# Two transformer layers on one core: aligned activation parts, a three-tile rotation for the last score pairs, and an output projection cut in two

## The chip, the cores and the metric

The kernel runs on one core of a Trainium2 chip. The metric is the device time of one execution in microseconds (us). Three runs of the kernel before gave 3531.59, 3531.69 and 3532.29 us; the median, 3531.69, stands for it below.

## The reference

Two identical layers work on a sequence of 2048 tokens with 512 features. Both layers use the same weights.

```python
# attention: 32 heads of 16 features
qkv = layernorm(x) @ wqkv                       # 512 x 1536
p = softmax(q @ k.T / sqrt(16)); o = p @ v
x = x + o.reshape(B, S, D) @ wo                 # 512 x 512
# MLP with Mish, hidden size 1792
h = layernorm(x) @ w1 + b1
x = x + (h * tanh(softplus(h))) @ w2
```

All of it is float32, and the softmax is a true one, with the maximum of each row taken off.

## The kernel before

**Precision.** The kernel gets float32 accuracy from a faster matmul form by splitting operands: each is a high part (rounded by a copy to the type `F32R`) and a low part (the rest). A product is three matmuls: high by high, high by low, low by high. `mm3` (L176 to L181) issues these three; so lines 179, 180 and 181 of the profile stand for the projections `qk`, `va`, `vp`, `wo` and `h`. The second MLP product `mo` issues its three at L724.

**Tiling.** The 2048 tokens are four chunks of 512 (index `c`). A layer runs through these stages:

1. `qkv`: query and key projections (`order` lists which feature block of which chunk comes when), then the value projection of chunks 0 to 2 (`v_parts`, 48 parts of three matmuls).
2. Attention: eight groups of four heads, four query chunks, 16 key tiles make 512 steps (`STEPS`) of four heads each.
3. Output projection `project(c)` of each chunk: 16 parts of three matmuls (`wo_parts`), added to the residual `x2s[c]` on VectorE (DVE) at L685, two row tiles at a time.
4. MLP: for each chunk and each of 14 hidden tiles, `hid(c, f)` computes a 128 x 512 tile of hidden values in 12 matmuls and sends it through ten operations that alternate between ScalarE (ACT) and DVE (L701 to L712); they end in the high part `ah` and the low part `al`. `outp(c, f)` multiplies these by `w2` in 12 matmuls (L724), with slices of `ah` and `al` as the stationary operand and `w2` as the moving one. `outp` trails `hid` by two groups (`LAG = 2`).

**The attention loop.** Per three steps, `CYCLE` holds four `P` (a pair of heads: two score matmuls into a PSUM tile of tag `s2`, one exponential of 128 x 1024 on ACT), four `S` (a single head: one score matmul into the PSUM tile `s1`, one exponential of 128 x 512), four `v` (probabilities by values: a run of narrow `pv` matmuls) and six `M` (the row maxima: two `pm` matmuls into one of two PSUM tiles of tag `mx`, one reduction on DVE at L387). `s2` and `s1` have one buffer each, so a pair's matmuls wait until the exponential of the pair before it has read `s2`. The maxima of a query chunk must be complete before its scores, so `M` runs ahead of `P`: `AHEAD + PRE` = 28 steps of maxima are issued inside stage 1 (`some_max`, after some projections and after every third value part); the first four steps of the loop have value projections of chunk 3 in place of `M`; and `M` is used up 24 steps before the end of the loop. From step 500 on (`FILL = 12`) each step also issues one part of `project(0)`; 16 steps hold all of it.

**What sets the order.** On TensorE the order is that of the code, written out by an explicit chain (`att.pe`). On the other engines a planner places an instruction where it believes its inputs to be ready, also ahead of others that stand before it in the code; `behind(...)` pins an instruction behind everything that its engine has been given so far. DMAs of the SP and POOL queues are issued in the order in which they are placed there, and one that waits holds up those behind it.

**Memory.** `blk` is a pool of 22 buffers of 8 KB per partition; weights, probabilities, residuals and normalised activations rotate through it. `tmp` is a pool of smaller tiles with a fixed place for each tag, in the order of first use. Adding up the sizes of the tiles that come ahead of them: every `blk` buffer starts at a multiple of 512 bytes; the tags `f` and `ah` of `tmp` start 384 bytes past a multiple of 512; `hr`, `he` and `al` start 128 bytes past one.

**The seam between attention and MLP.** After the loop come the loads of the last chunk's heads (`outs[3].load`), of residuals and weights; then `project(1)` with the first normalisation of chunk 0 between its parts, then `project(2)`, then the MLP. The last chunk's heads are divided by their softmax sums and split into parts at the hook of hidden tile 2 (`outs[3].parts(False)`: a multiplication of 128 x 2048 on DVE at L655, a copy on ACT, a subtraction on DVE at L662), and projected at tiles 6 to 9. The normalisations of the later chunks (`spread`, `norm_blocks`, `statistics`: L189, L278, L283 and two DMAs) are spread over hooks from tile 7 of chunk 0 and tile 5 of chunks 1 and 2. Their statistics are not pinned.

Of the kernel before, what the change touches and what calls it, by code (L numbers as in the profile page):

```python
# [18 lines left out]
P = 128  # L19
# [21 lines left out]
AHEAD = 24  # L41
PRE = 4
FILL = 12
# [6 lines left out]
LAG = 2  # L50
MAX_M = (6, 3, 7)
# [17 lines left out]
def kernel(ctx: ExitStack, tc: tile.TileContext, x, wqkv, wo, w1, b1, w2, out):  # L69
# [8 lines left out]
    dram = ctx.enter_context(tc.tile_pool(name="dram", bufs=1, space=DRAM))  # L78

# [103 lines left out]
    def statistics(src, nm):  # L183
        st = tmp.tile([P, NCH, 6], F32, tag="st", name=f"st{nm}")
        mv = tmp.tile([P, NCH, 2], F32, tag="mv", name=f"mv{nm}")
        ve = tmp.tile([P, NCH], F32, tag="ve", name=f"ve{nm}")
        rs = tmp.tile([P, NCH], F32, tag="rs", name=f"rs{nm}")
        for t in range(NCH):
            nc.vector.bn_stats(st[:, t], src[:, t])  # L189
# [114 lines left out]
    class Attention:  # L304
        def __init__(self, l, scr):
# [5 lines left out]
            self.singles, self.full, self.unit = 0, None, 0  # L311
            self.chained, self.last = False, None
# [50 lines left out]
        def max_mm(self, s, half):  # L363
            if s >= STEPS:
                return
# [56 lines left out]
        def pair(self):  # L422
# [4 lines left out]
            sp = self.pool.tile([P, 2, CW], F32, tag="s2", name=f"sp{self.l}{i}")  # L427
# [55 lines left out]
        def run(self, hooks, pre, fill):  # L483
# [3 lines left out]
            with tc.tile_pool(name="sa", bufs=1, space=PSUM, reuse_waits="tile") as self.pool:  # L487
                half, done = 2 * (AHEAD + PRE), -4
                for s in range(STEPS + 4):
# [21 lines left out]
                    if s + FILL >= STEPS:  # L511
                        next(fill, None)
# [21 lines left out]
    def qkv(l, att, wts, tt, order, within, due):  # L534
# [91 lines left out]
    class HeadsOut:  # L626
# [26 lines left out]
        def parts(self, aside):  # L653
# [4 lines left out]
            if aside:  # L658
                nc.gpsimd.tensor_copy(oh, self.num)
            else:  # L660
                nc.scalar.activation(oh, self.num, AF.Copy)
            behind(nc.vector.tensor_tensor(ol, self.num, oh.bitcast(F32), op=ALU.subtract))  # L662
            self.out = oh, ol

    def wo_parts(l, c, outs, wot, x2, pe, paired=True):
        oh, ol = outs[c].out
        for t in range(NCH):
# [15 lines left out]
            if paired and t % 2:  # L683
                x2v = x2[:, t - 1 : t + 1]
                behind(nc.vector.tensor_tensor(x2v, acc, x2v, op=ALU.add))  # L685

    def mlp(l, x2s, w1t, w2t, tts, dst, hooks, pe):
# [27 lines left out]
        def outp(c, f):  # L715
# [5 lines left out]
            turns = zip(*terms) if f == FT - 1 else [terms[0] + terms[1], terms[2]]  # L721
# [75 lines left out]
    for l in range(2):  # L797
# [18 lines left out]
        qkv(l, att, wts, tt, order, within, due)  # L816
        wot, w1t, w2t, x2s, tts = [], [], [], [], {}
# [24 lines left out]
        for i in range(2):  # L842
            at(STEPS - GSTEPS + 2 * i, lambda i=i: wot.append(ready(f"wo{i}", l)))
            at(STEPS - 50 + 2 * i, lambda i=i: load_res(i))
        at(STEPS - GSTEPS + 8, lambda: load_w1(0))
        outs = [HeadsOut(l, c, att.oscr) for c in range(NCH)]
        for c, (t0, t1, t2, t3) in enumerate(((-42, -20, -19, -13), (-26, -19, -18, -11), (-10, -6, -4, 0))):
# [4 lines left out]
            at(STEPS + t3, lambda o=o: o.parts(True))  # L852
# [4 lines left out]
        fill = project(0)  # L857
        att.run(hooks, v_parts(l, NCH - 1, wts, tt, att, True), fill)
# [5 lines left out]
        for _ in fill:  # L864
# [5 lines left out]
        for i, _ in enumerate(project(2)):  # L870
# [12 lines left out]
        on(2, lambda: outs[3].parts(False))  # L883
# [15 lines left out]
        if l == 0:  # L899
            last = NCH - 1  # L900
            for f, js in ((2, (0,)), (4, (2,)), (9, (1,)), (11, (3,)), (12, (4,)), (13, (5,))):
                hooks.setdefault((last, f), []).append(lambda js=js: load_qkv(1, wts, js, splits))
            for c in range(last):
                spread(hooks, last, (1, 5, 8)[c], x2s[c], f"q1{c}", tt, c)
        mlp(l, x2s, w1t, w2t, tts, xs if l == 0 else out, hooks, att.pe)
# [29 lines left out]
```

## Time and profile before

| what | value |
|---|---|
| median of three runs | 3531.69 us |
| profiled execution, its own time | 3532.86 us |
| its span, first to last instruction | 3531.1 us |
| TensorE busy (PE) | 3512.9 us, 28572 matmuls |
| VectorE busy (DVE) | 3002.7 us |
| ScalarE busy (ACT) | 2582.8 us |
| TensorE clock granted, mean | 0.999 |

Times within the profile are microseconds from the start of the span. Layer 0 has its attention loop from 164 to 1419 and its MLP from 1444 to 1777; layer 1 has them from 1920 to 3176 and from 3203 to the end. PE is the matmul stream, PEld the loading of the stationary operand, which runs beside the matmuls. Matmuls overlap in the pipeline: one of 512 columns lasts 389 ns in the profile, but the next one starts about 227 ns after it. So the cost of a matmul is read from one start to the next, not from its duration.

### The profile page before, as it was taken

The numbers are of one execution on the slowest core, as the hardware profiler recorded it, in microseconds if no ns is written. First come the engines' busy times: TensorE is split into PE (matmuls) and PEld (weight loads), VectorE is DVE, ScalarE is ACT, GpSimd is POOL, SyncE is SP. The second block draws the span as 40 slices with busy tenths as digits, with TensorE's granted clock in tenths as the row PEclk, the third lists the DMA queues.
The fourth block names the chain that finished last, engine by engine and source line by source line (L and its number), as shares of the span: only waits on it lengthen the run. The fifth ranks groups of instructions, "written<-read, shape, count | busy, mean of one in ns | idle before, by whom it ended". The sixth has DMA issues, their size and how long they took to land.

```text
span 3531.1 us, 68820 instructions
## 1 busy us (share of the span) xinstructions
PE 3512.9 (99%) x28572; PEld 1922.5 (54%) x28572; DVE 3002.7 (85%) x3160; ACT 2582.8 (73%) x3513; POOL 239.2 (7%) x392
## 2 busy tenths in 40 slices
PE   9999999999999999999999999999999999999999
PEld 7644444444444444788876444444444444447887
DVE  6789999999999994776756999999999999947665
ACT  3288888888888888356622888888888888874665
POOL 3100001010000002100010000000000000021000
PEclk9999999999999999999999999999999999999999
DMA  7641312213131124630364211112121111247100
GB/s 250 228 92 47 83 47 74 61 51 71 43 81 42 49 81 71 207 96 25 111 217 147 48 39 38 38 29 44 31 36 39 41 36 31 79 74 222 66 13 24
DMA packets 182196, 273.97 MB, mean 78 GB/s; under 512 B 67508, under 2 KB 111476, under 8 KB 168060
## 3 DMA queue, kind: packets, MB, share of 16 engines
q1 hardware_dynamic: 154964, 192.91, 21.4%
q10 hardware_dynamic: 19176, 43.06, 3.5%
q0 software_dynamic: 7744, 33.60, 3.4%
q8 instruction: 224, 3.67, 0.4%
q14 instruction: 88, 0.72, 0.1%
HBM read 158.87 MB, written 109.58 MB: 76 GB/s over the span
## 4 chain that ended last, share of the span: by engine, by line
PE 96%; DVE 2%; DMA 1%; issue 1%; ACT 0%; POOL 0%; SPq 0%; DVEq 0%; ACTq 0%; POOLq 0%
PE pv L457 30%; PE pm L383 18%; PE ss L441 13%; PE sp L431 10%; PE mo L724 8%; PE h L179 3%; PE h L181 3%; PE h L180 3%; PE qk L179 2%; PE qk L180 1%; PE qk L181 1%; PE wo L179 1%; PE va L179 1%; PE wo L181 1%; PE wo L180 1%
## 5 line engine op out<-in xcount | busy, mean ns | idle before, releaser
L387 DVE TENSOR_REDUCE mxv<-pm 128x2 f32<-128x1024 f32 x2048 | 2385.2, 1219 | 138.6 <-PE pm L383 88.5
L432 ACT ACTIVATE p<-sp 128x1024 f32<-128x1024 f32 x1366 | 1395.9, 1022 | 19.7 <-PE sp L431 15.3
L457 PE MATMUL pv<-p,va 128*32 128x256 f32 (+2 forms) x16032 | 1166.9, 392 | 0.1
L383 PE MATMUL pm<-ks,qs 48*128 48x512 f32 x4096 | 1096.0, 446 | 0.3
L442 ACT ACTIVATE p<-ss 128x512 f32<-128x512 f32 x1364 | 814.6, 597 | 349.1 <-PE ss L441 263.5
L431 PE MATMUL sp<-qs,ks 50*128 50x512 f32 x2732 | 725.6, 447 | 0.5 <-ACT p L432 0.2
L457 PEld LDWEIGHTS pv<-p,va 128*32 128x32 f32 x16032 | 367.7, 108 | 498.4 <-issue 420.6
L383 PEld LDWEIGHTS pm<-ks,qs 48*128 48x128 f32 x4096 | 449.9, 184 | 345.6 <-issue 216.6
L441 PE MATMUL ss<-qs,ks 50*128 50x512 f32 x1364 | 611.0, 448 | 0.0
L441 PEld LDWEIGHTS ss<-qs,ks 50*128 50x128 f32 x1364 | 252.0, 185 | 329.5 <-ACT p L442 225.5
L431 PEld LDWEIGHTS sp<-qs,ks 50*128 50x128 f32 x2732 | 261.1, 183 | 200.5 <-ACT p L432 119.1
L402 POOL CAST np<-nt 128x32 fp32r<-128x32 f32 x64 | 13.3, 208 | 2213.4 <-DVE nt L400 2213.4
L701 ACT ACTIVATE hb<-h,b1t 128x512 f32<-128x512 f32 x112 | 76.7, 685 | 96.6 <-PE h L181 90.6
L173 ACT ACTIVATE pt<-qk 128x512 fp32r<-128x512 f32 x64 | 38.2, 597 | 143.5 <-PE qk L181 102.9
L705 ACT ACTIVATE hr<-he 128x512 f32<-128x512 f32 x112 | 70.9, 633 | 82.3 <-DVE he L704 82.3
L708 DVE TENSOR_TENSOR hb<-hb,hr 128x512 f32<-128x512 f32 x112 | 77.2, 689 | 51.0 <-ACT hr L706 49.3
L712 DVE TENSOR_TENSOR al<-hb,ah 128x512 fp32r<-128x512 f32 x112 | 77.2, 690 | 36.8 <-ACT ah L711 33.8
L711 ACT ACTIVATE ah<-hb 128x512 fp32r<-128x512 f32 x112 | 70.5, 629 | 50.7 <-DVE hb L708 40.1
L702 DVE TENSOR_SCALAR he<-hb 128x512 f32<-128x512 f32 x112 | 47.5, 424 | 67.0 <-ACT hb L701 61.6
L704 DVE SCALAR_TENSOR_TENSOR he<-he 128x512 f32<-128x512 f32 x112 | 77.0, 687 | 25.4 <-ACT he L703 24.8
L703 ACT ACTIVATE he<-he 128x512 f32<-128x512 f32 x112 | 70.3, 628 | 32.2 <-DVE he L702 32.2
L174 DVE TENSOR_TENSOR pt<-qk,pt 128x512 fp32r<-128x512 f32 x64 | 43.9, 686 | 52.8 <-ACT pt L173 50.7
(235 smaller groups left out, 3081.8 us busy)
## 6 DMA issues: line engine op xcount, KB each, us to landing
scr<-pt ACTq DMA_DIRECT2D x64, 512.0 KB
qs<-scr SPq DMA_DIRECT2D x174, 128.0 KB
ks<-scr SPq DMA_DIRECT2D x174, 128.0 KB
vscr<-v SPq DMA_DIRECT2D x32, 512.0 KB
va<-vscr SPq DMA_DIRECT2D x64, 256.0 KB
oscr<-ot SPq DMA_DIRECT2D x64, 256.0 KB
ww<-sw POOLq DMA_DIRECT2D x14, 1024.0 KB, 4.9
num<-oscr SPq DMA_DIRECT2D x64, 128.0 KB
```

The lines of the kernel that those rows point to most:

```text
L179: pe(nc.tensor.matmul(acc, ah, bh, start=first and i == 0, stop=False))
L180: pe(nc.tensor.matmul(acc, ah, bl, start=False, stop=False))
L181: pe(nc.tensor.matmul(acc, al, bh, start=False, stop=last and i == n - 1))
L383: nc.tensor.matmul(pm[:, e], qs[u][rows, q0 : q0 + P], ks[u][rows, ts(n, 512)], start=True, stop=True)
L387: nc.vector.tensor_reduce(self.mxs[b][:, 2 * u : 2 * u + 2, qt, n], pm, axis=AX.X, op=ALU.max)
L431: self.pe(nc.tensor.matmul(sp[:, e], k, q, start=True, stop=True))
L432: nc.scalar.activation(self.pts[-1][:, 0:n], sp[:, 0:n], AF.Exp, scale=SCALE)
L441: self.pe(nc.tensor.matmul(sp, k, q, start=True, stop=True))
L442: nc.scalar.activation(self.pts[i // 3][:, 2], sp, AF.Exp, scale=SCALE)
L457: nc.tensor.matmul(self.accs[b][ts(h, VW), cols], self.va[b // NCH][:, kt, h, :], self.pts[j][:, e, cols], start=kt == 0 and q0 == 0, stop ...
L708: nc.vector.tensor_tensor(hb, hb, r, op=ALU.mult)
L724: nc.tensor.matmul(obs[c][t // 2][:, t % 2], act[:, ts(t, P)], w[:, part, f % 2], start=f == part == 0 and act is ah, stop=f == FT - 1 and ...
```

## The change

There are three groups of edits.

Addresses: two small tiles, 128 bytes (`gap0`, ahead of everything in `tmp`) and 256 bytes (`gap1`, ahead of the tags `hr`, `he`, `al`), move `f` and `ah` by 128 bytes and `hr`, `he` and `al` by 384, so that all of them start at multiples of 512.

The end of attention: `AHEAD` goes from 24 to 22, so 26 steps of maxima lie in stage 1 and `M` is used up 22 steps before the end; in the value projection the maxima come after parts 2, 5, 8 and so on instead of 3, 6, 9. From the first `M` that has nothing left to do, the pairs take their PSUM tile in turn from `mx`, `mx` and `s2`. `project(0)` is no longer spread over the last steps: all of it follows the loop. The loads of `wo`, of two residuals and of the first `w1` tile move from 64 to 50 steps before the end to 9 to 1 steps before it.

The seam: `project(2)` stops after 10 of its 16 parts; three parts follow the first `hid`, the other three the second. Its last addition is not pinned. The last chunk's heads are handled in four half-size pieces at hidden tiles 2 to 5, not in one at tile 2. The statistics of all spread normalisations are pinned. (`terms` in `outp` is the same sequence of matmuls as before.)

```diff
-AHEAD = 24
+AHEAD = 22
-FILL = 12
+HEAD = 10
...
+    tmp.tile([P, 32], F32, tag="gap0", name="gap0", bufs=1)
...
         for t in range(NCH):
-            nc.vector.bn_stats(st[:, t], src[:, t])
-            nc.vector.bn_aggr(mv[:, t], st[:, t])
+            behind(nc.vector.bn_stats(st[:, t], src[:, t]))
+            behind(nc.vector.bn_aggr(mv[:, t], st[:, t]))
...
         def max_mm(self, s, half):
             if s >= STEPS:
+                self.idle = self.idle or 1
                 return
...
         def pair(self):
...
-            sp = self.pool.tile([P, 2, CW], F32, tag="s2", name=f"sp{self.l}{i}")
+            spare = self.idle and self.idle % 3
+            self.idle += self.idle > 0
+            pool, tag = (ps, "mx") if spare else (self.pool, "s2")
+            sp = pool.tile([P, 2, CW], F32, tag=tag, name=f"sp{self.l}{i}")
...
-                    if s + FILL >= STEPS:
-                        next(fill, None)
...
-                if i % 3 == 0:
+                if i % 3 == 2:
                     some_max()
...
+        def pieces(self):
+            nm = f"{self.l}{self.c}"
+            oh = b8([P, KT, CW], F32R, "oh" + nm)
+            ol = b8([P, KT, CW], F32R, "ol" + nm)
+            self.out = oh, ol
+            for u in range(2):
+                two = ts(u, KT // 2)
+                behind(nc.vector.tensor_tensor(self.num[:, two], self.num[:, two], self.rec[:, two], op=ALU.mult))
+                nc.scalar.activation(oh[:, two], self.num[:, two], AF.Copy)
+                yield
+            for u in range(2):
+                two = ts(u, KT // 2)
+                behind(nc.vector.tensor_tensor(ol[:, two], self.num[:, two], oh[:, two].bitcast(F32), op=ALU.subtract))
+                yield
...
-                behind(nc.vector.tensor_tensor(x2v, acc, x2v, op=ALU.add))
+                ins = nc.vector.tensor_tensor(x2v, acc, x2v, op=ALU.add)
+                if c < 2:
+                    behind(ins)
...
                 hid(c, f)
+                for _ in range(3 + i):
+                    next(rest, None)
...
+        if l == 0:
+            tmp.tile([P, 64], F32, tag="gap1", name="gap1", bufs=1)
...
-            at(STEPS - GSTEPS + 2 * i, lambda i=i: wot.append(ready(f"wo{i}", l)))
-            at(STEPS - 50 + 2 * i, lambda i=i: load_res(i))
-        at(STEPS - GSTEPS + 8, lambda: load_w1(0))
+            at(STEPS - 9 + 2 * i, lambda i=i: wot.append(ready(f"wo{i}", l)))
+            at(STEPS - 5 + 2 * i, lambda i=i: load_res(i))
+        at(STEPS - 1, lambda: load_w1(0))
...
-        for c, (t0, t1, t2, t3) in enumerate(((-42, -20, -19, -13), (-26, -19, -18, -11), (-10, -6, -4, 0))):
+        for c, (t0, t1, t2, t3) in enumerate(((-42, -21, -20, -14), (-26, -20, -19, -12), (-10, -6, -5, 0))):
...
-        for _ in fill:
+        for _ in project(0):
             pass
...
-        for i, _ in enumerate(project(2)):
+        last = project(2)
+        for i in range(HEAD):
+            next(last)
...
-        on(2, lambda: outs[3].parts(False))
+        pieces = outs[3].pieces()
+        for f in range(2, 6):
+            on(f, lambda: next(pieces))
```

More of the change, by code (lines that the diff above doesn't have):

```diff
@@ L481, in drain, with run @@
             nc.sync.dma_start(self.oscr[qb][g // 2, g % 2], ot)
-        def run(self, hooks, pre, fill):
+        def run(self, hooks, pre):
             self.prep_v(0, range(NCH - 1))
@@ L899 @@
         if l == 0:
-            last = NCH - 1
+            end = NCH - 1
             for f, js in ((2, (0,)), (4, (2,)), (9, (1,)), (11, (3,)), (12, (4,)), (13, (5,))):
[L902 to L905, printed above, removed]
+                hooks.setdefault((end, f), []).append(lambda js=js: load_qkv(1, wts, js, splits))
+            for c in range(end):
+                spread(hooks, end, (1, 5, 8)[c], x2s[c], f"q1{c}", tt, c)
+        mlp(l, x2s, w1t, w2t, tts, xs if l == 0 else out, hooks, att.pe, last)
     close_banks()
```

17 lines of the change are left out of this document (7 added, 10 removed).

## The prediction

> **What bounds the kernel.** I read the page's busy times first, then its chain of work that ended last.
>
> ```profile
> PE 3512.9 (99%) x28572; PEld 1922.5 (54%) x28572; DVE 3002.7 (85%) x3160; ACT 2582.8 (73%) x3513; POOL 239.2 (7%) x392
> PE 96%; DVE 2%; DMA 1%; issue 1%; ACT 0%; POOL 0%; SPq 0%; DVEq 0%; ACTq 0%; POOLq 0%
> ```
>
> TensorE is the bound from end to end. So the change can gain in three ways only: matmuls that follow each other more closely, less idle time, less matmul time added by the way things are interleaved. Next I looked for idle time, in the waits of PE and in the windows around the seams.
>
> ```profile
> PE mo L724 <- ACT ah L711: 5.7, 3, 2.2
> PE vp L179 <- DVE mxv L387: 1.7, 2, 0.9
> PE mo L724 <- DVE al L712: 0.3, 1, 0.3
> ...
> 1446.00:1480.00 34.00, 30.43 (x125) 24.12 (x124) 29.87 (x49) 20.14 (x30) 5.33 (x10) 0.95 0.85 246
> 3172.00:3206.00 34.00, 33.63 (x163) 25.82 (x162) 25.75 (x45) 3.68 (x6) 7.11 (x13) 1.00 0.80 259
> 3206.00:3236.00 30.00, 27.48 (x118) 21.54 (x117) 26.61 (x42) 20.05 (x30) 3.52 (x6) 1.00 0.83 224
> ```
>
> The waits give total, count and longest in us; the windows give length, then busy time of PE, PEld, DVE, ACT and POOL, granted clock, DMA share and GB/s. At the start of each MLP the first `mo` waits for its activations while DVE is about 88% busy. In layer 0 the clock is also halved for a moment: 0.95 over 34 us is 1.7 us lost.
>
> **Part A, addresses.** I compared spacings from start to start: a clean run of `wo` matmuls by the timeline, then the MLP by the chain, whose pieces give start and length.
>
> ```profile
> 3176.40 0.39 PE L179 MATMUL wo<-wo0l,oh 128*128 128x512 f32 x1
> ...
> 3184.33 0.39 PE L181 MATMUL wo<-wo1l,ol 128*128 128x512 f32 x1
> ...
> 1777.31 2.33 PE mo L724 x10
> ...
> 3262.05 2.80 PE mo L724 x12
> ...
> 3506.49 2.79 PE mo L724 x12
> ...
> L724 PEld LDWEIGHTS mo<-w25l,ah 128*128 128x128 f32 x128 | 24.1, 188 | 5.5
> ...
> L180 PEld LDWEIGHTS wo<-wo1l,oh 128*128 128x128 f32 x64 | 12.1, 188 | 1.7
> ```
>
> The first two rows are 35 matmuls apart: 7.93 / 35 = 226.6 ns. The rows at 3262.05 and 3506.49 are 44 groups of 24 matmuls (12 `h`, 12 `mo`) apart: 5.555 us per group. At 226.6 ns it would be 5.438, so 0.117 us per group is lost; the `mo` half itself runs at 2.80 / 12 = 233 ns. `wo` has the same shape and a stationary operand cut in the same slices; what differs is that `oh` starts at a multiple of 512 bytes and `ah` and `al` don't. The other difference, that `mo` changes its PSUM bank at each matmul, is answered by the row at 1777.31: there, at the last hidden tile (L721), three in a row go to one bank, and the spacing is 233 ns again. I take the full gain: 0.117 x 107 groups (the first groups, with stalls, left out) = 12.5 us. Bounds: 0, if the spacing has another cause, and 13.1 with all 112 groups; a loss has no row. The weak point is the last two rows: the load itself shows the same 188 ns for both operands.
>
> The Trainium skill, SBUF — State Buffer, section "Specifications (TRN2)", states that the memory's lines are 16 bytes and that only stepping to a new line costs. Offsets of 384 and 128 are whole lines, so by that page this part gives 0 and the sum below is 12.5 higher; no run here has timed another offset yet, and the spacings above speak against the page's line being the only unit.
>
> **Part B, the seam into the MLP.** These are rows of PE and DVE there, by the timeline.
>
> ```profile
> 3208.62 0.39 PE L181 MATMUL h<-thm,w11l 128*128 128x512 f32 x1
> 3211.17 1.20 PE L724 MATMUL mo<-w20l,ah 128*128 128x512 f32 x4 [2.16 <-ACT ah L711]
> ...
> 3197.20 1.29 DVE L189 BATCH_NORM_STATS2 stm<-x 128x6 f32<-128x512 f32 x2
> 3200.88 1.23 DVE L685 TENSOR_TENSOR x<-wo,x 128x1024 f32<-128x1024 f32 x1 [1.29 <-PE wo L181]
> ...
> 3204.15 1.25 DVE L189 BATCH_NORM_STATS2 stm<-x 128x6 f32<-128x512 f32 x2
> ...
> 3222.68 2.29 DVE L655 TENSOR_TENSOR num<-num,rec 128x2048 f32<-128x2048 f32 x1
> 3227.61 2.29 DVE L662 TENSOR_TENSOR ol<-num,oh 128x2048 fp32r<-128x2048 f32 x1
> ```
>
> `mo` starts 2.55 us after the matmul before it, 2.32 more than the usual spacing. Four times 0.16 us of pipeline overlap (389 - 227 ns) turn the 6.0 us of waits on `ah` and `al` into about 6.7 us of lost time, and the halved clock adds 1.7: 8.4 us in all. Statistics of the next chunk's normalisation (L189), due at hidden tile 7, have been placed ahead of the first hidden tiles' DVE work. Pinning removes them from here and, since L278 and L283 need their result, those too. The six parts of `project(2)`, 18 x 0.2266 = 4.1 us, now stand between the first `hid` and the first `mo`, against a wait of 2.16. The pieces hold DVE for half of 2.29 at a time. So both sides of the wait move the right way. The last addition of `project(2)` (1.23 on DVE) now lies behind the second `hid`, and the first `mo` needs its PSUM tile: it has the third `hid`, 12 x 0.2266 = 2.72, to finish in. I take 8.0: 0.4 for `h`, which now starts three parts (2.0 us) after the last transposes where it had nine (6.1). New DVE load: tile 7 gets four statistics, about 2.6 us, against `mo`'s lead of two groups, 11 us; that hides them. Bounds: 0 (the wait only moves, to `h` or to the pinned pieces behind late `rec`) and 8.4.
>
> By the Trainium skill, TensorE: Matmul & The Clock Gate, section "What's actually happening", the clock falls after about 3.4 us of idleness. The trace disagrees, since 2.2 us was enough in layer 0 and the same wait was not in layer 1; by the page 1.7 us would not belong to this wait, and the sum would be 1.7 higher.
>
> **Part C, `AHEAD`.** One step of maxima in the value projection costs this much of PE:
>
> ```profile
> 1880.09 0.39 PE L181 MATMUL va<-qkv4l,tlq 128*128 128x512 f32 x1
> 1880.41 0.73 PE L383 MATMUL pm<-ks,qs 48*128 48x512 f32 x4
> 1881.07 0.50 PE L179 MATMUL va<-qkv4l,thq 128*128 128x512 f32 x1
> 1881.41 0.39 PE L180 MATMUL va<-qkv4l,thq 128*128 128x512 f32 x1
> ```
>
> From 1880.09 to 1881.41 lie 1.32 us where two matmuls take 0.45: 0.87, with the next few slightly slow 0.89. Two steps fewer in each of two layers: 3.6 us less. The wait of `vp` on `mxv` (1.7 in all) goes, because the last maxima now end seven parts before it. The first maxima of the value projection come a part (0.68) earlier, while DVE still works on those before: up to 0.68 each, 1.3. Net 4.0; bounds 2.3 and 5.3. The two steps come back in the loop, and are counted there. `P` then follows its maxima by two steps (4.8 us) less; six steps, 14 us, stay for the fold and its two small DMAs.
>
> **Part D, the last steps of attention.** Here are a normal loop, the stretch without `M`, and the stretch with the fill.
>
> ```profile
> 3099.67 0.50 PE L441 MATMUL ss<-qs,ks 50*128 50x512 f32 x1
> 3106.90 0.49 PE L441 MATMUL ss<-qs,ks 50*128 50x512 f32 x1
> ...
> 3115.26 0.49 PE L441 MATMUL ss<-qs,ks 50*128 50x512 f32 x1
> 3115.72 0.49 PE L431 MATMUL sp<-qs,ks 50*128 50x512 f32 x2
> 3116.15 0.85 PE L457 MATMUL pv<-p,va 128*32 128x384 f32 x8
> 3116.93 0.49 PE L441 MATMUL ss<-qs,ks 50*128 50x512 f32 x1
> ...
> 3161.47 0.50 PE L441 MATMUL ss<-qs,ks 50*128 50x512 f32 x1
> 3161.48 0.72 PE L431 MATMUL sp<-qs,ks 50*128 50x512 f32 x2
> 3162.13 0.86 PE L457 MATMUL pv<-p,va 128*32 128x256 f32 x16
> 3162.92 0.50 PE L441 MATMUL ss<-qs,ks 50*128 50x512 f32 x1
> ...
> 3114.65 1.02 ACT L432 ACTIVATE p<-sp 128x1024 f32<-128x1024 f32 x1
> 3115.78 0.60 ACT L442 ACTIVATE p<-ss 128x512 f32<-128x512 f32 x1
> 3116.32 1.02 ACT L432 ACTIVATE p<-sp 128x1024 f32<-128x1024 f32 x1
> 3169.04 1.02 ACT L432 ACTIVATE p<-sp 128x1024 f32<-128x1024 f32 x1
> ```
>
> Three normal steps, four pairs, take 3106.90 - 3099.67 = 7.23: 1.81 us per pair. Without `M` a pair takes 3116.93 - 3115.26 = 1.67, and the pair's matmuls start 0.46 after the single's: they wait for `s2`. ACT too idles 0.11 between 3115.67 and 3115.78. Where nothing waits (3161.47 to 3162.92), PE needs 1.45 per pair. ACT needs 1.02 + 0.60, less 0.06 of overlap at each border: 1.50. With three tiles I take 1.50; bounds 1.45 and 1.67.
>
> From 3114.65 (pair 651 of a layer, step 488, where `M` ended) to `project(1)` at 3176.40 it took 61.75 us, `project(0)` included. Now: two steps with `M`, 2.3 pairs x 1.81 = 4.2; 28.7 pairs x 1.50 = 43.0; 3.0 from the last exponential to the end of `pv` (three `pv` runs of 0.79 and one of 1.0 follow the last pair, which now runs ahead of its exponential); `project(0)`, no longer covered by anything, 48 x 0.2266 = 10.9 and 0.1 at the border. Sum 61.2: 0.5 less per layer, 1.0 in both. Bounds: at 1.67 per pair 28.7 x 0.17 = 4.9 more per layer, so 8.8 slower in all; at 1.45, 3.9 faster.
>
> The five moved loads are 1 MB each, 5.2 MB. At the 259 GB/s of the window from 3172 that is 20 us. They are issued from step 503 on; `project(0)` starts some 9 x 2.0 + 4 = 22 us later and needs the two of `wo` at once, the rest later (`w1` 32 us later). So I cost them at nothing, with the pool of 22 buffers and SP's order as the risk. The inversions, broadcasts (POOL queue) and splits of the earlier chunks move by one step of 2 us, to where `M` has just left DVE; their results are needed 10.9 us later than before or more, so they cost nothing either.
>
> **Sum.** 12.5 + 8.0 + 4.0 + 1.0 = 25.5 us. The profiled execution took 3532.86, 1.76 more than its span; the median is 3531.69. 3531.69 - 25.5 = 3506.2, rounded to 3506.
>
> **Rivals.**
> - *The address is not the cause.* For it: equal 188 ns of weight load. Against it: `wo` and `mo`. Then only B, C and D: 3531.7 - 13.0 = 3519. The rule of the Trainium skill named in part A would come out here.
> - *The pairs don't speed up.* The single `s1` tile, or ACT, holds 1.67 per pair, and the freed `project(0)` costs its full time: 3506 + 9.8 = 3516. For it: 1.45 and 1.50 lie so close that any wait shows.
> - *The seam's wait moves*, to the first `h` or to DVE behind late `rec`: 3514.
> - *Slower: `wo` late.* SP issues in order, and a load that waits for one of 22 buffers holds those behind it. If `wo` lands more than 12.8 us after the loop's end in each layer, 25.6 in all, the gain is gone; 17 us late gives 3540. Against it: 22 us of lead for 8 us of transfer.
> - *No change at all* needs two of these together.
>
> **Chances.** Forecast 0.62 (own range 3499 to 3512), address not the cause 0.15, pairs not faster 0.10, wait moved 0.06, late `wo` 0.05, 0.02 for mixtures within 0.2%. About 0.2%, 7 us, is what a measurement tells from no change; faster means below 3524.6. The first four cases are faster, less some mixtures: 0.91, 0.04 and 0.05. The range 3498 to 3521 takes in the forecast's own range, the first rival and the next two.
>
> **What would show it.** A: `h` and `mo` at 227 ns, 5.44 per group. B: no wait of `mo` on `ah`, clock 1.00 in layer 0's seam. C: no wait of `vp`. D: 1.50 per pair and an ACT without gaps after step 490, `project(0)` in 10.9 us at once. Wrong would be: groups still at 5.55, pairs at 1.67, or PE idle ahead of `wo`.

## The result and the profile after

| kernel | median us | lowest to highest, executions | against the kernel before |
|---|---|---|---|
| before | 3532.15 | 3531.59 to 3533.14, 6 | 1 |
| changed | 3546.97 | 3542.96 to 3552.18, 6 | 1.0043, 95% interval 1.003 to 1.0056 |

The changed kernel is slower by 0.43%, where 3506 us was forecast. Its profiled execution took 3551.37 us with a span of 3549.6, 18.5 more than the span before. First the busy times of its page:

```profile
PE 3503.1 (99%) x28572; PEld 1932.6 (54%) x28572; DVE 3003.6 (85%) x3164; ACT 2578.2 (73%) x3515; POOL 242.9 (7%) x392
```

TensorE is busy for 10 us less, although the halved clock described below lengthens its matmuls, and the span is longer: its idle time has grown from 18.2 to 46.5 us. The waits of PE (total us, times, longest) show where:

```profile
PE mo L742 <- ACT ah L729: 13.0, 4, 4.6
PE ss L447 <- ACT p L448: 11.0, 4, 5.5
PE wo L182 <- DVE ol L678: 6.9, 2, 3.4
PE wo L180 <- DVE x L701: 3.6, 2, 2.6
PE pm L386 <- DVE mxv L390: 1.6, 2, 0.8
```

The wait of `mo` that part B was to remove has grown from 5.7 to 13.0 us, and three large new ones stand below it: of `ss` (the score matmul of a single head; `sp` are those of a pair) in the last steps, of `project(3)` on `ol`, and of `project(1)` on `x`. `project(3)` is issued in four quarters of four parts, one behind each of hidden tiles 6 to 9. The windows add what the clock did there (columns as in the prediction):

```profile
1353.00:1424.00 71.00, 62.16 (x555) 28.64 (x550) 22.53 (x17) 47.42 (x66) 24.43 (x41) 0.95 0.67 146
1444.00:1542.00 98.00, 89.66 (x379) 73.00 (x378) 59.08 (x97) 46.73 (x73) 5.37 (x10) 0.97 0.50 152
1694.00:1777.00 83.00, 77.05 (x326) 62.59 (x325) 67.52 (x127) 45.79 (x74) 5.83 (x6) 0.96 0.42 123
3121.00:3191.00 70.00, 64.21 (x555) 29.30 (x547) 22.18 (x17) 47.28 (x65) 24.44 (x41) 0.93 0.69 148
3211.00:3310.00 99.00, 91.70 (x379) 74.43 (x378) 59.08 (x98) 46.67 (x73) 5.38 (x10) 0.93 0.48 149
```

The granted clock is 0.93 to 0.97 in each stage with a long wait. The clock's record has 46.1 us at half speed, against 6.0 before; half of them, about 20 us more, is lost. Here is where the time lies, from starts of instructions in the traces, in us for layer 0 / layer 1. The last column is taken from two later runs, e8 for the first row and e9 for the others, which have the delays found below removed:

| stage | before | changed | delays removed |
|---|---|---|---|
| pair 651 to the start of `project(1)` | 68.5 / 68.5 | 71.1 / 70.4 | 61.0 / 62.3 |
| `project(1)` to the first `h` | 24.3 / 24.3 | 19.8 / 19.8 | 19.7 / 19.8 |
| first 14 groups of the MLP | 88.6 / 86.2 | 98.2 / 99.2 | 86.3 / 86.3 |
| MLP, chunks 1 and 2 | 155.9 / 155.6 | 152.3 / 152.3 | 153.6 / 152.3 |
| MLP, chunk 3 to the last `h` | 74.9 / 74.7 | 82.8 / 73.2 | 74.9 / 73.2 |

Chunks 1 and 2 show the gain alone. The last steps, the first 14 groups and layer 0's chunk 3 give it back. Now the timeline of the changed kernel at these places:

```profile
3130.75 0.49 PE L447 MATMUL ss<-qs,ks 50*128 50x512 f32 x1
...
3139.42 0.50 PE L447 MATMUL ss<-qs,ks 50*128 50x512 f32 x1
...
1390.39 2.29 DVE L659 TENSOR_TENSOR num<-num,rec 128x2048 f32<-128x2048 f32 x1 [6.19 <-DMA num<-oscr]
...
1392.77 1.02 ACT L438 ACTIVATE p<-sp 128x1024 f32<-128x1024 f32 x1 [5.57 <-DVE num L659]
...
1397.84 2.20 SPq L844 DMA_DIRECT2D x<-in_A_x_dram  x2
1418.43 0.34 SPq L164 DMA_DIRECT2D w10l<-ww  x1
1418.87 0.38 SPq L644 DMA_DIRECT2D num<-oscr  x1
...
1426.38 2.87 SPq L641 DMA_DIRECT2D den<-oscr  x4
...
1462.39 0.69 DVE L730 TENSOR_TENSOR al<-hb,ah 128x512 fp32r<-128x512 f32 x1 [0.76 <-ACT ah L729]
1470.97 1.23 DVE L673 TENSOR_TENSOR num<-num,rec 128x1024 f32<-128x1024 f32 x1 [7.89 <-DMA rec<-rscr]
1472.12 0.42 DVE L720 TENSOR_SCALAR he<-hb 128x512 f32<-128x512 f32 x1
...
1765.81 2.19 ACT L295 ACTIVATE thq<-tlq 128x512 fp32r<-128x512 f32 x4 [4.38 <-DMA tlq<-ntq]
1767.90 0.61 ACT L721 ACTIVATE he<-he 128x512 f32<-128x512 f32 x1
```

- *Last steps.* The first two rows are six pairs apart: 8.67 / 6 = 1.445 us per pair, so three PSUM tiles do what they were for. Then an exponential waits 5.57 us, not for PE but for DVE's multiplication of chunk 1 at 1390.39: by the code, its buffer for `p` is the one in which chunk 1's broadcast `rec` lies until then.
- *SyncE's queue.* Between 1400 and 1418 it issues nothing. The first `w1` load (`w10l`) stands at its head and starts when DVE has ended chunk 2's multiplication (1416.11 + 2.29). Chunk 3's `num` and `den` stand behind it.
- *Hidden tiles.* `rec` of chunk 3 lands late: its eight broadcasts are issued from 4.8 us behind the first `h` on, where it was 1.5, and take up to 18.3 us to land, where it was 12.1. The first piece, pinned on DVE, waits 7.89 us for it. Behind it waits `he` of a hidden tile (L720), and so `ah`, and so `mo`.
- *Layer 0, chunk 3.* A normalised chunk's copy on ACT (L295) waits 4.38 us for its DMA with `he` behind it.

### The profile page after: what moved, and what is told of

The parts are those of the page before. It is cut to its first block, busy times and chain, and to the rows that moved or that the text cites. A ratio compares the mean times of both kernels' runs of the same rounds, so it can differ in the third digit from the quotient of the medians.

```text
span 3549.6 us, 68828 instructions
## 1 busy us (share of the span) xinstructions
PE 3503.1 (99%) x28572; PEld 1932.6 (54%) x28572; DVE 3003.6 (85%) x3164; ACT 2578.2 (73%) x3515; POOL 242.9 (7%) x392
## 5 line engine op out<-in xcount | busy, mean ns | idle before, releaser
L438 ACT ACTIVATE p<-sp 128x1024 f32<-128x1024 f32 x1366 | 1395.7, 1022 | 18.4 <-DVE num L659 10.2
L437 PE MATMUL sp<-qs,ks 50*128 50x512 f32 x2732 | 741.5, 445 | 0.0
L437 PEld LDWEIGHTS sp<-qs,ks 50*128 50x128 f32 x2732 | 270.4, 184 | 184.2 <-ACT p L438 110.2
L719 ACT ACTIVATE hb<-h,b1t 128x512 f32<-128x512 f32 x112 | 77.1, 689 | 94.3 <-PE h L182 91.7
L729 ACT ACTIVATE ah<-hb 128x512 fp32r<-128x512 f32 x112 | 70.4, 629 | 57.5 <-DVE hb L726 44.3
L720 DVE TENSOR_SCALAR he<-hb 128x512 f32<-128x512 f32 x112 | 47.6, 425 | 75.0 <-ACT hb L719 74.4
```

What stands on the lines that cost most here:

```text
L437: self.pe(nc.tensor.matmul(sp[:, e], k, q, start=True, stop=True))
L438: nc.scalar.activation(self.pts[-1][:, 0:n], sp[:, 0:n], AF.Exp, scale=SCALE)
L719: nc.scalar.activation(hb, acc, AF.Identity, bias=b1t[:, f : f + 1])
```

## The experiments

Each run has the kernel before beside it on its chip, with medians of 3534 to 3536 us; ratios are to those. "Changed" stands at 1.0043.

### The addresses alone, and three single edits

**e1**, the kernel before with the two gap tiles:

```diff
 (before)
+    tmp.tile([P, 32], F32, tag="gap0", name="gap0", bufs=1)
...
+        if l == 0:
+            tmp.tile([P, 64], F32, tag="gap1", name="gap1", bufs=1)
```

> The kernel before with nothing but the two gap tiles. In the changed kernel the MLP groups run at 5.44 us where they ran at 5.555, so if the address alone does that, this kernel gains about 12 us: 3520 against 3532, with h and mo at 227 ns. Rival: the closer spacing came from the new order around the MLP; then this kernel stays at 3532 and its groups at 5.55.

Measured 3527.1 us, 0.9972 (0.9961 to 0.9983): 9 us faster, and the rival is out. The largest of its waits:

```profile
PE mo L725 <- ACT ah L712: 8.0, 5, 2.2
```

The matmuls close up as expected (chunks 1 and 2 take 153.6 and 152.4 us), and 2.3 us of that is waited for elsewhere: `mo` now waits 8.0 us for `ah` against 5.7.

**e2**, the changed kernel with the five loads at their old steps:

```diff
-            at(STEPS - 9 + 2 * i, lambda i=i: wot.append(ready(f"wo{i}", l)))
-            at(STEPS - 5 + 2 * i, lambda i=i: load_res(i))
-        at(STEPS - 1, lambda: load_w1(0))
+            at(STEPS - GSTEPS + 2 * i, lambda i=i: wot.append(ready(f"wo{i}", l)))
+            at(STEPS - 50 + 2 * i, lambda i=i: load_res(i))
+        at(STEPS - GSTEPS + 8, lambda: load_w1(0))
```

> The changed kernel with the five loads (wo, two residuals, first w1) issued 64 to 50 steps before the end, as before. Theory: the late loads are what delays the last chunk's chain, since the first w1 load waits on SP for a buffer that a DVE multiplication frees, and everything behind it lands late; then the waits of mo and wo in hidden tiles 2 to 5 (4.8 + 3.6 us in layer 0, 3.7 + 3.6 in layer 1) and the halved clock after them (about 10 us) go, and the kernel falls to about 3521. Rival: the late loads don't matter, because the stall comes from the faster end of attention or from the pieces; then it stays within 3540 to 3550. The stall of a pair's exponential behind the multiplication of chunk 1 (6 us per layer) is expected to stay by both, since a score buffer still follows a broadcast in the same place.

Measured 3547.22 us, 1.003 (1.002 to 1.004): the theory's 3521 failed, the rival's range held. The first 14 groups fall to 90.0 / 92.8 us, and the last steps take that back: the exponential at 1377 us now waits for chunk 0's multiplication, and the clock stays halved for 34.1 us behind it.

**e3**, only the first `w1` load moved, behind the loads of chunk 3:

```diff
-        at(STEPS - 1, lambda: load_w1(0))
...
         outs[3].load()
+        load_w1(0)
```

> The changed kernel with one load alone moved: the first w1 tile is issued right after the last chunk's heads are loaded instead of one step before the end of the loop. Theory that this one load, waiting on SP, holds up the queue for 18 us: den and num of chunk 3 are issued about 12 us earlier, the weights behind them too, the broadcasts land by about 1460 instead of 1470, and the MLP stalls in hidden tiles 2 to 5 go: 3521, as with all five. Rival (all five loads share the blame, through the traffic): less than 8 us gained. Rival (pieces): nothing gained.

Measured 3538.79 us, 1.0009 (0.9999 to 1.0018), 12 us better than the changed kernel by the ratios, 8 by the medians.

```profile
PE mo L742 <- ACT ah L729: 4.9, 2, 3.8
```

This view is chunk 3's eight broadcasts, first in the changed kernel, then in e3:

```profile
DMA to landing us min/median/max: 7.0/13.1/18.3
```

```profile
DMA to landing us min/median/max: 6.7/7.4/7.4
```

They land at most 7.4 us after their issue where they took 18.3, and the first 14 groups take 91.5 / 91.6. So the place of this one load in the queue costs time, and is a part only. How it does so is not what was expected: the broadcasts are issued no earlier (4.5 us behind the first `h`, against 4.8). What became short is their landing. The weight loads behind `w10l` start 11 us earlier by the first `h` (`w11l` at 1425.7, against 1432.3), so less of that traffic is left when the broadcasts start; that this is the reason was not tried by itself.

**e4**, the statistics not pinned:

```diff
-            behind(nc.vector.bn_stats(st[:, t], src[:, t]))
-            behind(nc.vector.bn_aggr(mv[:, t], st[:, t]))
+            nc.vector.bn_stats(st[:, t], src[:, t])
+            nc.vector.bn_aggr(mv[:, t], st[:, t])
```

> The changed kernel with the statistics of the spread normalisations not pinned. Theory that pinning is what makes layer 0's last chunk stall (1.4 + 1.3 + 3.7 us and 3.4 us by the clock): chunk 3 of layer 0 goes from 82.8 us back to 73 to 75, and the start of the MLP is not worse; about 3537. Rival: that stall comes from elsewhere (the transfers of the normalised block); then chunk 3 keeps 82.8 and the time stays at 3547; or the statistics, placed early again, cost at the seam what they save here.

Measured 3529.17 us, 0.9983 (0.9974 to 0.9992): about 20 us better than the changed kernel, the largest gain of a single edit.

```profile
PE ss L447 <- ACT p L448: 9.9, 3, 4.8
PE wo L182 <- DVE ol L678: 5.3, 4, 1.5
```

`mo` has left the list, the first 14 groups take 89.7 / 89.4, and layer 0's chunk 3 is back at 73.2 from 82.8. The wait in the last steps is untouched. In layer 0 the first piece of chunk 3 starts even later than in the changed kernel, but DVE no longer waits for it:

```profile
1471.97 1.18 DVE L673 TENSOR_TENSOR num<-num,rec 128x1024 f32<-128x1024 f32 x1
```

SyncE's queue is as blocked as before (`w10l` starts at 1419.1), and the broadcasts are issued no earlier. With the statistics free, the next chunk's normalisation (L190, L279, L284) stands ahead of the piece on DVE and fills the time in which it would have waited; the broadcasts themselves land within 8.2 us, by 1462.0.

### Two delays away, and what is left

The next four all have the edits of e3 and e4. **e5** has nothing else; **e7** also has the quarters two groups later; **e8** also has chunk 0 earlier:

```diff
 (e7)
-        for f in range(6, 10):
+        for f in range(8, 12):
             on(f, quarter)
 (e8)
-  ((-42, -21, -20, -14), (-26, -20, -19, -12), (-10, -6, -5, 0))
+  ((-42, -32, -31, -20), (-26, -21, -20, -12), (-10, -6, -5, 0))
```

> The changed kernel with the statistics of the norms not held to their place and the first w1 load put behind the loads of chunk 3. Theory (both delays act in the first 14 groups of the MLP, where each alone took 7 to 10 us off, and cannot be taken off twice): only some 1 to 3 us per layer below the 3529 us of the kernel with free statistics, 3523 to 3528 us; the stage of the first 14 groups at about 87 us from 89.5. Rival (the two delays are independent): another 8 us, 3521 us or less. Both: the wait of the p exponential for chunk 1's multiply (5 us in each layer) and the halved clock behind it stay.

Measured 3526.74 us, 0.9977 (0.9967 to 0.9986). Like e4, within both intervals, and the first 14 groups take 89.5 / 89.4 as there: the two delays act at the same place and don't add.

> As the run with both delays taken away, with the four quarters of project(3) two groups later, after hidden tiles 8 to 11 in place of 6 to 9. Theory (they wait for the pieces of chunk 3, 3.5 us in each layer): the two gaps of 1.5 to 1.9 us in each layer go, 5 to 7 us faster than without the move. Rival (the pieces are late by themselves and hold VectorE's order): the gaps move with the quarters or to a mo group; same time within 1.5 us.

Measured 3518.89 us, 0.9949 (0.9932 to 0.9965), 8 us below e5 where 5 to 7 were expected; the waits on `ol` are gone and the first 14 groups take 86.3 / 86.3.

> As the run with both delays taken away, with chunk 0's inversion, spread and parts at steps -32, -31 and -20 and chunk 1's spread as it was, so that chunk 1's reciprocals do not queue behind chunk 0's eight broadcasts. Theory (the 5 us wait of the p exponential, and 7 to 14 us of halved clock behind it, come from chunk 1's broadcast landing late): broadcast of chunk 1 lands 6 us earlier, the PE gap of 5 us near 1389 and 3141 us is gone, and 8 to 16 us in the two layers together come off: 3509 to 3518 us. Rival (the next buffer, chunk 2's or chunk 0's, waits in its place): a gap of 3 us or more stays in the last 20 steps, within 3 us of the run without the move.

Measured 3515.23 us, 0.9957 (0.9928 to 0.9986), executions from 3509.01 to 3537.78. By these times alone e8 is not told apart from e5, whose interval overlaps; the profile of its fastest execution shows what the edit does. This view is e8's broadcasts between 1360 and 1385, where the changed kernel has 16 with up to 10.6 us to landing:

```profile
L655 POOL DMA_DIRECT2D rec<-rscr x8: 512/512/524, 1364.4 to 1368.0; - x8
...
DMA to landing us min/median/max: 3.5/5.0/6.5
```

Chunk 1's land by 1374.5 in place of 1390.0, nothing over 1.5 us is waited for in the last steps, and the stage up to `project(1)` takes 61.0 / 62.3 us. The stall was chunk 1's broadcast: its reciprocals are written out by GpSimd's queue, behind chunk 0's eight.

**e6**, e5 with part D undone (fill of 12 steps, two PSUM tiles, old steps of the projection's loads and of the inversions):

```diff
+FILL = 12
...
-            pool, tag = (ps, "mx") if spare else (self.pool, "s2")
-            sp = pool.tile([P, 2, CW], F32, tag=tag, name=f"sp{self.l}{i}")
+            sp = self.pool.tile([P, 2, CW], F32, tag="s2", name=f"sp{self.l}{i}")
...
+                    if s + FILL >= STEPS:
+                        next(fill, None)
```

> As the run with both delays taken away, with all of part D taken back: the 12 parts of project(0) again between the last steps, the pairs on their two own PSUM tiles, the projection's loads and the inversions at their old steps. Theory (part D gives nothing here: the pairs' 10 us per layer go to project(0) alone, 10.9 us, and the wait for chunk 1's multiply comes on top with its halved clock): 2 to 8 us faster than the run with part D, 3517 to 3523 us, no gap over 3 us between the last 20 steps and the first w1 group. Rival (part D pays and the wait only hides it): slower than with part D by 1 us or more.

Measured 3543.95 us, 1.0021 (1.0011 to 1.003): 16 us slower than e5 by the medians, so the theory fell and part D pays. The two profiles understate it: that of e5 is its slowest execution, 3536.14 us, with 23.9 us of halved clock in the last steps of each layer. From pair 651 to the first `h` of layer 0 they are alike (93.3 us against 94.3 with part D); the first 14 groups take 94.4 / 95.7 against 89.5 / 89.4, with a new wait on DVE:

```profile
1472.96 1.30 DVE L285 STREAM_TRANSPOSE ym<-xnm 128x512 f32<-128x512 f32 x2 [4.53 <-DMA ntm<-ym]
```

A transpose of the next chunk's normalisation waits for the DMA that empties its buffer `ym`, and holds the hidden tile. With `project(0)` spent, less TensorE work lies between chunk 3's loads and the MLP; whether this is the reason was not tried by itself.

### All four away

**e9** has the edits of e3, e4, e7 and e8. **e11** is e8 with the seam of the kernel before (but for the last addition of `project(2)`, which stays unpinned); **e10** is the changed kernel with chunk 0 earlier, **e12** with the pieces and the quarters two tiles later.

```diff
 (e11)
-        for i in range(HEAD):
-            next(last)
+        for i, _ in enumerate(last):
...
-        pieces = outs[3].pieces()
-        for f in range(2, 6):
-            on(f, lambda: next(pieces))
+        on(2, lambda: outs[3].parts(False))
 (e10: chunk 0 as in e8)
 (e12)
-        for f in range(2, 6):
+        for f in range(4, 8):
             on(f, lambda: next(pieces))
...
-        for f in range(6, 10):
+        for f in range(8, 12):
             on(f, quarter)
```

> The changed kernel with all four delays taken away: statistics free, the first w1 load behind the loads of chunk 3, chunk 0 inverted, spread and split earlier, the quarters of project(3) two groups later. Theory (the four are separate in place: chunk 3 of layer 0, SyncE's queue, the last steps, hidden tiles 6 to 9): the gains add, so the kernel with the first three (3515 us, its undisturbed profile 3509) less 3 us per layer: 3501 to 3510 us, no PE gap over 3 us in the last 20 steps or in the MLP, under 5 us of halved clock. Rival (one wait only uncovers the next): no faster than 3515 us.

Measured 3513.68 us, 0.9949 (0.9932 to 0.9966), the fastest median of all; executions from 3504.61 to 3537.12, six of the twelve under 3509 and so within the theory's range. No wait of PE is over 1.5 us, as expected, but the profiled execution, the slowest, has 83.4 us of halved clock where under 5 were expected. By the ratios e9 is no faster than e7 (0.9949 for both), which lacks the earlier chunk 0. So in the time the gains don't all add; the section on the hardware looks at that clock.

> As the run with the first three delays taken away, with the form of the seam taken back to that of the kernel before: project(2) whole ahead of the first w1 group, chunk 3 split in one piece behind hidden tile 2, the ah and al terms of an output group in two blocks in place of three. Theory (the seam's part is worth the 8 us that the forecast gave it once its two delays are gone): slower than the run with all four taken away by 5 to 11 us, 3509 to 3520 us, with PE gaps of 2 to 2.6 us before the first mo groups. Rival (the seam's gain was never there): within 2 us of that run or faster.

Measured 3519.92 us, 0.9979 (0.9957 to 1.0001), 6 us above e9 by the medians, with intervals that overlap. By the profiles `project(1)` to the 15th group takes 112.0 / 109.6 against e9's 105.9 / 106.0. Against e8, whose quarters stand at tiles 6 to 9 as in e11, it is 109.2 / 109.3: the seam's form alone brings 3 us, the form and the moved quarters together 9.6.

> The changed kernel with only chunk 0's inversion, spread and parts moved earlier. Theory (the wait of the p exponential for chunk 1's multiply costs its 5 us gap and half of the clock's halved time behind it in each layer, whatever the MLP does): the last stage of the attention falls from 57 to 48 us in each layer, the delays of the MLP stay, 3525 to 3535 us against the 3547 of the changed kernel. Rival (steps that end earlier only meet the blocked SyncE queue and chunk 3's late loads): the gain comes back as a longer stage behind it, 3540 us or more.

Measured 3558.4 us, 1.0054 (1.0029 to 1.008), executions from 3532.37 to 3575.92. Three of the ten lie in the theory's range, the median far above it. The profiled one has 44.4 and 34.1 us of halved clock from 1341 and 3116 us on.

> The changed kernel with only the four pieces of chunk 3 two groups later (hidden tiles 4 to 7) and the quarters two groups later (8 to 11). Theory (the pieces are kept in VectorE's order behind a broadcast that lands 8 us late, and what stands behind them there holds the hidden tiles): the PE gaps of 5.0 and 4.0 us at the second output group and of 3.8 us at the quarters go, with 3 to 7 us of halved time per layer: 14 to 20 us faster than the changed kernel, 3527 to 3533 us. Rival (the statistics of the next chunk, kept in the same order behind tile 7, are what holds the tiles): one of the gaps stays at 3 us or more, 3538 us or more.

Measured 3535.65 us, 1.0004 (0.9995 to 1.0013), 14 us better than the changed kernel by the ratios. The wait at the second output group is gone, the two of 3.4 us on `ol` are not. These are rows of DVE at the first of them, which ends at 1492.07:

```profile
1490.80 1.22 DVE L678 TENSOR_TENSOR ol<-num,oh 128x1024 fp32r<-128x1024 f32 x1
1491.93 0.69 DVE L190 BATCH_NORM_STATS2 stm<-x 128x6 f32<-128x512 f32 x1
```

The quarter waits for the last `ol`, since pieces and quarters kept their distance. The pinned statistics stand behind that `ol` and don't hold it. So the gap that the rival expected stayed, but not for the rival's reason.

### The last steps by another way, and the addresses once more

**e13** is e9 with chunk 0 at the changed kernel's steps and its broadcasts on SyncE's queue; **e14** is e13 without the gap tiles; **e15** is the changed kernel with only the queue edit:

```diff
-                behind(nc.gpsimd.dma_start(self.rec[ts(h, DH)], rows[:, h][None].to_broadcast([DH, KT, CW])))
+                low = nc.gpsimd if self.c else nc.sync
+                behind(low.dma_start(self.rec[ts(h, DH)], rows[:, h][None].to_broadcast([DH, KT, CW])))
```

> As the run with all four delays taken away, but chunk 0's inversion, spread and parts stay at the changed kernel's steps (-21, -20, -14), and its eight broadcasts are issued on SyncE's queue in place of GpSimd's. Theory (chunk 1's reciprocals and broadcast queue behind chunk 0's on GpSimd's queue, and the 1.36 us gap of the earlier inversion is what halved the clock for some 40 us in part of the executions): no gap at 1339 us, chunk 1's broadcast lands by 1380 us, the 5 us gap at 1389 us is gone, 3500 to 3508 us with all runs within 8 us. Rival (the halved clock in the steps with maxima came by itself): again runs above 3520 us.

Measured 3518.92 us, 0.9952 (0.994 to 0.9965), executions from 3516.07 to 3520.05. The spread is gone, as expected; the time is missed by 11 us.

```profile
PE wo L180 <- DVE x L702: 10.8, 2, 7.3
PE ss L447 <- ACT p L448: 4.4, 2, 3.1
```

Chunk 1's broadcasts land at 1381 where 1380 was expected, `ss` still waits up to 3.1 us for an exponential, and what the steps win `project(1)` waits for: its PSUM tile needs an addition that stands on DVE behind chunk 2's `num` and `ol`. The Trainium skill, DMA: Bandwidth & Descriptors, section "Issuing engines are not separate DMA queues", says that another issuing engine saves only issue time, which it calls usually small beside the transfer. The trace agrees that the transfers share what carries them: the eight of chunk 1 took up to 12.2 us to land in layer 0 and 13.3 in layer 1, where they took 10.6 and 9.8 in the changed kernel. The issue time was not small here: in layer 0 they were issued 9 to 10 us earlier, and the last landed 8.8 us earlier.

> The changed kernel with only chunk 0's eight broadcasts on SyncE's queue. Theory (the last steps' stall with its clock is worth 8 us per layer whatever the MLP does): the last steps take 48 us in each layer in place of 57, the MLP's delays stay, 3527 to 3534 us against 3547, no run above 3540. Rival (what the steps win is waited for at the blocked SyncE queue): 3540 us or more.

Measured 3543.4 us, 1.0022 (1.0012 to 1.0032), 7 us better than changed by the ratios. The last steps take 50.1 / 54.5 us up to the last `pv`, and `project(1)` then waits 6.9 and 1.8. So the rival's range held, and part of what the steps win is indeed waited for, but at `project(1)` for an addition on DVE and not at SyncE's queue.

> As the run with chunk 0's broadcasts on SyncE's queue, without the two gap tiles, so that the activation parts lie as in the kernel before. Theory (the spacing of 227 ns against 233 ns of the h and mo matmuls lies on the path wherever nothing else waits): 9 to 13 us slower than that run. Rival (part of it is taken back by waits of the hidden tiles' chain): 3 to 8 us slower.

Measured 3527.95 us, 0.998 (0.9971 to 0.9989): 9.0 us slower than e13 by the medians, as expected. By the profiles the MLP (first `h` to last `h`) takes 318.3 / 317.8 against 313.1 / 311.8: 11.2 us.

## Why the prediction was wrong, point by point

**Part A was right in its cause and somewhat large.** These are rows of the chain in the changed kernel:

```profile
3503.43 2.72 PE mo L742 x12
...
3525.19 2.72 PE mo L742 x12
```

They are four groups apart: 5.44 us per group, and 2.72 / 12 = 227 ns for `mo`. The rows of the stage table in which nothing waits give 3.6 + 3.3 + 1.5 us; e1 and e14 give 9 us by medians. e14's MLPs give 11.2 by the profiles. So 12.5 was the size of the cause, of which waits take back 1 to 3.5. That it works through the stationary operand of `mo` is not shown: `h` closed up too, from (5.555 - 2.80) / 12 = 229.6 ns to 226.7, and its operands lie in `blk` buffers, which the gap tiles don't move. The rival by the 16-byte line of SBUF — State Buffer in the Trainium skill, section "Specifications (TRN2)", is out: 128 and 384 bytes are whole lines, and 9 us came of them.

**Part B failed at two sentences and left one wait out.** "That hides them", of the statistics at tile 7, priced only chunk 0 and only by DVE's time; e4 shows the pins worth some 20 us, half of it in layer 0's chunk 3, which the working never visits. And "the pinned pieces behind late `rec`" was named as a bound of 0; it was no bound, since a pinned wait can last longer than the wait it replaces: 7.89 us on DVE against 2.16 on PE. The wait left out is that of the quarters: the pieces were priced by DVE's time alone, but the last `ol` now comes behind tile 5, and the first quarter, at tile 6, waits for it: 6.9 us over both layers in the changed kernel, and e7 gains 8 us by moving the quarters. The size of 8.0 was reached only with that further edit: in e9 the second and third stage of the table together save 6.9 us in layer 0 and 4.5 in layer 1, of which some 2.8 are part A's (24 groups by 0.117). In e8, with the quarters in place, it is 3.6 and 1.3, which leaves 2.1.

**Part C was about right.** Of the 2.0 us taken for each layer, 0.9 is the wait of `vp`, which stands behind the first scores and is gone. The rest, 1.1, is the change of the start up to the first scores. It came in layer 1 (-1.1, of which 0.2 is part A's) and not in layer 0 (+0.2), where the warm-up matmuls, transposes and `qk` took 1.0 us longer, which this part doesn't touch. One wait of `pm` on `mxv` came, 1.6 us in all, which had been bounded at 1.3. No run had this part alone.

**Part D had a wrong row and two wrong noughts.** The row at 3114.65 was called pair 651. By a count of the exponentials of the kernel before from there to the end, and from 3107.9:

```profile
L432 ACT ACTIVATE p<-sp x28: 1016/1024/1033, 3114.6 to 3169.0; 128x1024 f32<-128x1024 f32 x28
...
L432 ACT ACTIVATE p<-sp x32: 1016/1024/1033, 3107.9 to 3169.0; 128x1024 f32<-128x1024 f32 x32
```

it is pair 655, four later. The stretch that took 61.75 took 68.47 from pair 651, and the forecast of 61.2 for the new one was good: 61.0 and 62.3 in e8. So the part was worth 13.6 us over both layers and not 1.0. The noughts are those of the broadcasts ("so they cost nothing either") and of the five loads. The pairs became faster, so each buffer came round sooner, and the broadcast that lay in one did not (e8, e13). It even came later: from the start of pair 651 to the landing of chunk 1's last broadcast it took 27.6 and 27.1 us before, and 37.0 and 35.7 in the changed kernel. Of the loads the risk was named and laid at `wo`, which came in time (`project(0)` begins 0.5 us after the start of the last `pv`); `w10l` was the load that held the queue (e3). The wait of `project(1)` for the addition to `x` (3.6 us) is in no line of the prediction.

**The clock was left out.** The prediction counted 1.7 us of halved clock to be gained and none to be lost. Each long wait of the changed kernel brought a new stretch of it, about 20 us lost in all.

**The rivals.** The slower one had the right mechanism, a load that waits for a buffer and holds those behind it, with the wrong load, and no rival joined several waits with the clock. That 3506 lies among the lower executions of e9 is luck: e9 has edits that the forecast did not have, and part D was worth 12.6 us more than it was given.

## What to carry to other kernels

When a stretch is made faster, go through the rotating buffers that it uses: whoever still reads one of them, a broadcast or a late multiplication, is the next bound, and so is every queue entry behind a load that takes such a buffer. A pin behind a DMA is safe only if the DMA's landing has been checked against the pinned place, since the whole engine waits with it. Price a wait of TensorE above 3 us with the halved clock that followed nearly all of them here.

## What the runs showed of the hardware

- *Addresses.* With the start of `f`, `ah`, `hr`, `he` and `al` moved to multiples of 512 bytes, `mo` goes from 233 to 227 ns and `h` from 230 to 227, while the weight load shows 188 ns in both. Which of the tiles counts, and by what, is open: `ah` and `al` are stationary operands of `mo`, in the MLP the others are touched by ACT and DVE alone, and nothing that `h` reads has moved. Other offsets were not tried.
- *The clock.* In the changed kernel every PE wait over 3.4 us (seven) was followed, 2.3 to 4.8 us after it began, by half speed for 3.4, 6.8 or 10.2 us; none of its four shorter ones above 0.9 was, the start apart. That is no sharp bound: over the profiles of all kernels here, 42 of the 46 waits above 3 us were followed so within 5.5 us, and 14 of the 69 between 0.9 and 3 us (2.16 us in the kernel before, 1.30 in e6). In the steps with maxima 0.97 us could be enough. With chunk 0 inverted earlier (e8 to e11), one such wait arises per layer. Here are the wait by the timeline and the window behind it, first of e8, then of e9:

```profile
1340.79 0.51 PE L437 MATMUL sp<-qs,ks 50*128 50x512 f32 x2 [0.97 <-ACT p L438]
```

```profile
1339.00:1379.00 40.00, 38.83 (x394) 16.24 (x390) 26.69 (x22) 36.98 (x51) 14.11 (x25) 1.00 0.62 99
```

```profile
1340.42 0.50 PE L437 MATMUL sp<-qs,ks 50*128 50x512 f32 x2 [0.97 <-ACT p L438]
```

```profile
1339.00:1379.00 40.00, 39.03 (x223) 15.62 (x221) 24.79 (x21) 21.57 (x28) 10.83 (x20) 0.53 0.44 71
```

  The waits are alike; in e9 the clock then stays at half for 37.5 us with PE busy in 39.0 of the 40, and 223 matmuls are done in place of 394. The profiles of e8 to e11 have eight such waits, four of them with a halved clock of 34 to 44 us. Half of that in each layer would account for the spread of those kernels' executions, 29 to 44 us; e13 to e15, without the wait, spread over 4 to 9 us. The Trainium skill, TensorE: Matmul & The Clock Gate, section "What's actually happening", has windows of about 3.4 us that run freely, and the clock back after one busy window. The lengths here agree with the first, being multiples of 3.41; the 37.5 us disagree with the second. What keeps the clock down that long is open.
- *Open.* `project(1)` waits for the addition to `x` in e7 and e8 too (5.8 and 2.4 us in layer 1). e9's gap at 1339 and this wait in e13 were not removed together, so the time of a kernel with neither was not measured.
